# Exchanging the last two rounds of token blocks in an attention-and-experts kernel

## The chip, the cores and the metric

The kernel runs on one core of a Trainium2 chip. The metric is the device time of one execution in microseconds (us); a kernel's figure is the median of its runs. The engines are named as in the profile: PE is TensorE's matmul, PEld its weight load, DVE is VectorE, ACT is ScalarE, POOL is GpSimd, SP is SyncE (SPq is its DMA queue).

## The reference

A short convolution over time with softmax weights (7 taps, 8 heads) feeds a mixture of 8 experts. Every one of the 14336 tokens goes to its two best experts by noisy logits, and the two results are added with softmax weights:

```python
x = attn_out.reshape(B * S, D)                       # 14336 x 192
noisy_logits = x @ w_gate + np.log1p(np.exp(x @ w_noise)) * noise
top2 = np.argpartition(-noisy_logits, 2, axis=1)[:, :2]
...
h = np.maximum(x[mask] @ w1[e], 0.0)                 # 192 -> 1024
out[mask] += top2_w[mask, k, None] * (h @ w2[e])     # 1024 -> 192
```

## The kernel before

**Front end.** Tokens come in 14 chunks of 1024. For each chunk the kernel loads x, computes the convolution (DVE), splits it into a high and a low fp16 part, computes the gate logits (PE), picks the two experts, and scatters each token's record into the queues of its two experts in HBM (`xg`), with 16 indirect DMAs from POOL (line 411).

**Rounds.** After chunk c has been queued, round c takes one block of rows from each of the 8 experts' queues. `ROUNDS` lists the rounds as pairs (chunk after which the round may run, rows of a block). A queue gets 256 rows per chunk on the average, so there are 14 rounds of 256-row blocks; a fifteenth round of 128-row blocks takes what is left over. Where a queue holds fewer rows than a block, the block reaches back over rows that were taken already, and those are sent to spare rows behind the output. Whatever then remains would go through a loop of 128-row blocks (`leftovers`), which makes no pass on this data.

**One block.** SP loads the block's records (`metas`, 8 small DMAs per round, line 817) and its transposed rows (`rows`, tile xT, line 823; six buffers). A block has 8 slices of 128 hidden units, taken several at a time so that each step fills a 128x512 PSUM tile: four steps of two slices for a 256-row block, two steps of four slices for a 128-row block. Each step is: first layer on PE into pm (line 879), relu to fp16 on ACT (hi, line 894), the rest pm - hi on DVE (lo, line 898), second layer on PE into py (line 919). PE's program has the first layer run up to three steps ahead of the second. py is one PSUM tile per block, with **two buffers**: block n uses the buffer of block n-2. A 256-row block has two halves of 128 rows side by side in its py, called a and b below.

**Finishing a block.** For each half in turn, `finish` scales py by the gate into an SBUF tile y (ACT, line 931; six y buffers) and adds y into the output with an indirect accumulating DMA from POOL (line 936, behind a small memset, line 935). The adds of one block may follow each other at once; a block's first add waits until the adds of the block before have landed, since a token can be in both.

**What sets the order.** Nothing is scheduled on the chip. `Sched` runs every work stream as a generator that yields (engine, estimated us, function, what it depends on), keeps a clock per engine from these estimates, and writes the instructions into the engines' programs in the order in which it picks them. The engines then run these fixed programs in order, with semaphores between them. In `finish` the planner reaches the scale of half b only when it has placed the add of half a on POOL, so a planned backlog of POOL moves the scale of b down in ACT's program:

```python
ty = yield ("ACT", act(D) + 0.07, scale, [t0, ("g", o.c, o.e)] + ...)
if t == o.nt - 1:
    T["y", bi] = ty
ta = yield ("POOL", 1.85, add, [ty + (AL if o.c else 0.0), ...] + before("added", bi, 1), 0.27)
```

Below, the blocks of the round of 128-row blocks are M0 to M7, and those of the last round of 256-row blocks L0 to L7.

Of the kernel before, what the change touches and what calls it, by code (L numbers as in the profile page):

```python
# [33 lines left out]
NC = NJ // CH  # L34
PARTS = [[(0, 4), (4, 4)]] + [[(0, CH)]] * (NC - 1)
GT = 4
ROUNDS = [(c, 256) for c in range(NC)] + [(NC - 1, 128)]
BMAX = 256
RBUF = 3
NTM = BMAX // P  # L40
# [107 lines left out]
def moe_kernel(ctx, tc, x_lay, wgen, noise, wgn, w1, w2, xg, out):  # L148
# [25 lines left out]
    def dve(n):  # L174
        return (n / 0.96 + 155) / 1e3
# [60 lines left out]
    def before(key, i, n):  # L236

        return [(key, i - n)] if i >= n else []
# [198 lines left out]
    def routing(c):  # L437
# [106 lines left out]
        d = dve(8)  # L544
        for q, (cc, b) in enumerate(ROUNDS):
            if cc != c:
# [16 lines left out]
    def strays(q, t):  # L563

        V = nc.vector
        nt = ROUNDS[q][1] // P
        S = [P, E, nt]
# [214 lines left out]
    steps, blist = [], []  # L782
    for c, (_, b) in enumerate(ROUNDS):
        for e in range(E):
# [12 lines left out]
    def prologues():  # L797

        for c, (k, b) in enumerate(ROUNDS):
            base = []  # L800
# [40 lines left out]
    def gates(c, tm):  # L841

        nt = ROUNDS[c][1] // P
        S = [P, E, nt]
# [77 lines left out]
    def finish(bi, t0):  # L922
# [3 lines left out]
        for t in range(o.nt):  # L926
# [21 lines left out]
            if t == o.nt - 1:  # L948
                T["y", bi] = ty
            ta = yield ("POOL", 1.85, add, [ty + (AL if o.c else 0.0), ("clear", ROUNDS[o.c][0]), ("token", o.c)] + before("added", bi, 1), 0.27)  # L950
            T["add", n] = ta + 2.2
# [184 lines left out]
```

## Time and profile before

| | |
|---|---|
| median of 3 runs | 1201.41 us (1190.59 to 1201.69) |
| profiled execution | 1206.64 us, of which the span of the profile is 1204.7 us |
| PE busy | 1051.8 us, 87% of the span |
| DVE, ACT, POOL busy | 825.7 us (69%), 526.0 us (44%), 749.8 us (62%) |
| granted TensorE clock, mean | 0.95 |
| adds into the output (line 936) | 232, 1759 ns each |

The span runs from the first to the last instruction of the profiled execution; the execution's own time is 1.94 us longer. Busy shares are averages over the whole span: the first 100 us are loading and weight preparation, and the last 14 us have almost no PE work.

### The profile page before, as it was taken

Reading aid. Unit: us, or ns where it says so; the run is one execution under the profiler, and the core shown is the slowest. Engines: PE = TensorE matmul, PEld = TensorE weight load, DVE = VectorE, ACT = ScalarE, POOL = GpSimd, SP = SyncE. Lnnn points to the kernel's source line nnn. Section 1 sums busy time; section 2 is a strip of 40 time slices with the busy share of each in tenths; the row PEclk is TensorE's granted clock in tenths of the full one; section 3 lists DMA queues with packets and bytes.
Section 4 is the critical chain, followed back from the end, with each engine's and each line's share of the span. In section 5 each row is a group of like instructions: output and inputs, shape, how many; then the busy total and the mean of one; then the engine's idle time right before and its main releaser. Section 6 shows DMA issues by size and latency. Waiting matters only on the chain.

```text
span 1204.7 us, 27979 instructions
## 1 busy us (share of the span) xinstructions
PE 1051.8 (87%) x10862; PEld 953.8 (79%) x10862; DVE 825.7 (69%) x1552; ACT 526.0 (44%) x1191; POOL 749.8 (62%) x1013
## 2 busy tenths in 40 slices
PE   1414899797998999999999999989999889999995
PEld 0201499786997999889999889879898779999995
DVE  5898878686795969778887859678885343333331
ACT  6868573342443444443435344434343233333332
POOL 0004368477686868778684858778787867434333
PEclk9755999898998999999999999999999989999998
DMA  9993473665647577485748666365555545434341
GB/s 246 244 283 100 117 170 62 92 145 95 132 88 138 109 125 98 88 161 96 154 78 155 107 117 129 58 131 120 79 91 81 102 74 81 52 54 47 35 41 21
DMA packets 249686, 132.48 MB, mean 110 GB/s; under 512 B 182096, under 2 KB 242000, under 8 KB 247888
## 3 DMA queue, kind: packets, MB, share of 16 engines
q1 hardware_dynamic: 205392, 85.37, 32.3%
q0 software_dynamic: 44160, 45.31, 24.9%
q8 instruction: 85, 1.39, 0.5%
q14 instruction: 49, 0.40, 0.1%
HBM read 38.70 MB, written 58.10 MB: 80 GB/s over the span
## 4 chain that ended last, share of the span: by engine, by line
PE 52%; POOL 15%; DMA 10%; DVE 7%; issue 6%; ACT 6%; SPq 4%; another core or an unknown queue 0%; POOLq 0%; DVEq 0%; ACTq 0%
PE pm L879 27%; PE py L919 24%; POOL xg L411 8%; POOL out L936 7%; DMA xt<-x_lay 3%; DMA out<-y,token 3%; SPq L817 2%; DVE acc L337 2%; DVE tmp L327 2%; DVE lo L898 2%; DMA xg<-rec,pos 1%; DMA xT<-xg 1%; DMA wres<-w 1%; ACT junk L682 1%; ACT junk L273 1%
## 5 line engine op out<-in xcount | busy, mean ns | idle before, releaser
L879 PE MATMUL pm<-xT,wres 128*128 128x256 f16 (+1 forms) x4800 | 594.3, 271 | 30.2 <-DMA xT<-xg 23.4
L936 POOL DMA_INDIRECT out<-y,token x232 | 408.0, 1759 | 254.4 <-ACT y L931 89.3
L898 DVE SCALAR_TENSOR_TENSOR lo<-pm,hi 128x512 f16<-128x512 f32 x464 | 316.1, 686 | 301.1 <-ACT hi L894 261.4
L879 PEld LDWEIGHTS <-wres 128*128 128x128 f16 x4800 | 451.6, 99 | 83.4 <-DMA xT<-xg 21.9
L919 PE MATMUL py<-wres,hi 128*128 128x192 f16 x3712 | 503.3, 247 | 9.8 <-ACT hi L894 4.0
L894 ACT ACTIVATE hi<-pm 128x512 f16<-128x512 f32 x464 | 275.7, 596 | 507.4 <-PE pm L879 407.7
L919 PE MATMUL py<-wres,lo 128*128 128x192 f16 x1856 | 458.6, 247 | 4.5 <-issue 3.0
L919 PEld LDWEIGHTS <-hi 128*128 128x128 f16 x3712 | 341.6, 98 | 23.2 <-issue 8.9
L411 POOL DMA_INDIRECT xg<-rec,pos x224 | 292.0, 1304 | 76.4 <-issue 67.5
L919 PEld LDWEIGHTS <-lo 128*128 128x128 f16 x1856 | 182.3, 98 | 8.5 <-issue 5.5
L337 DVE TENSOR_TENSOR acc<-acc,tmp 128x1536 f32<-128x1536 f32 (+1 forms) x90 | 148.0, 1644 | 1.1
L327 DVE TENSOR_TENSOR tmp<-xt,wt 128x1536 f32<-128x1536 f32 (+1 forms) x90 | 148.2, 1646 | 0.7
L931 ACT ACTIVATE y<-py,gate 128x192 f32<-128x192 f32 x232 | 96.3, 417 | 78.0 <-PE py L919 37.6
L935 POOL MEMSET spacer<- 1x1 f32 x232 | 102.8, 443 | 0.1
L533 POOL TENSOR_SCALAR rec<-rr 128x8 f32<-128x8 f32 x14 | 3.2, 229 | 90.7 <-DVE rr L482 89.8
L410 POOL MEMSET spacer<- 1x1 f32 x224 | 53.3, 238 | 0.1
L273 ACT ACTIVATE junk<-xt 128x192 f16<-128x192 f32 x118 | 42.3, 359 | 23.9 <-DMA xt<-x_lay 22.0
L602 PE MATMUL sums<-ss,ones 128*128 128x2 f32 x32 | 8.1, 333 | 39.4 <-ACT junk L682 39.4
L602 PEld LDWEIGHTS sums<-ss,ones 128*128 128x128 f32 x32 | 7.1, 282 | 43.0 <-ACT junk L682 43.0
L739 PE MATMUL sums<-wres,dg 128*128 128x512 f32 (+1 forms) x48 | 29.3, 698 | 5.3 <-ACT wres L743 3.1
L352 DVE TENSOR_TENSOR rec<-acc,rec 128x512 f16<-128x512 f32 (+2 forms) x30 | 26.8, 900 | 3.1 <-ACT rec L348 2.7
L739 PEld LDWEIGHTS sums<-wres,dg 128*128 128x128 f32 x48 | 9.9, 230 | 22.3 <-ACT wres L743 10.4
(139 smaller groups left out, 514.8 us busy)
## 6 DMA issues: line engine op xcount, KB each, us to landing
xt<-x_lay SPq DMA_DIRECT2D x13, 1344.0 KB
out<-zrec SPq DMA_DIRECT2D x14, 768.0 KB
wres<-w SPq DMA_DIRECT2D x6, 768.0 KB
out<-y,token POOLq DMA_INDIRECT x232
xg<-rec,pos POOLq DMA_INDIRECT x224
wt<-wgen SPq DMA_DIRECT2D x14, 224.0 KB
wres<-w SPq DMA_DIRECT2D x6, 512.0 KB
wres<-w SPq DMA_DIRECT2D x12, 256.0 KB
```

The source lines that it names most:

```text
L273: nc.scalar.activation(q, xtile[s][:, i - first], AF.Square, accum_out=nrm[:, i:i + 1])
L327: V.tensor_mul(tm[key].rearrange("p j (h g) -> p j h g", h=H), xt[:, t:t + n].rearrange("p j (h g) -> p j h g", h=H), w[:, a:a + n].rearra ...
L337: ta = yield ("DVE", cc, lambda: V.tensor_add(tm["acc"], tm["acc"], tm["tmp"]), [])
L410: nc.gpsimd.memset(spacer, 0.0)
L411: i = nc.gpsimd.indirect_dma_start(out=xg, out_offset=bass.IndirectOffsetOnAxis(ap=idx, axis=0), in_=src, in_offset=None)
L879: nc.tensor.matmul(dst, w[:, c0:c0 + 128], m, start=i == 0, stop=i == 4)
L894: nc.scalar.activation(h[0][:, :n], pm[:, :n], AF.Relu)
L898: T["lo", si] = yield ("DVE", dve(n), lambda: nc.vector.scalar_tensor_tensor(h[1][:, :n], pm[:, :n], 0.0, h[0][:, :n], op0=OP.max, op1=OP. ...
L919: nc.tensor.matmul(dst, h[:, cols], w[:, c0:c0 + D], start=begin, stop=f == F // P - 1 and i == 2, skip_group_check=True)
L931: nc.scalar.activation(y[0], o.py[t // 2][:, (t % 2) * D:(t % 2 + 1) * D], AF.Copy, scale=gate_of[o.c][:, o.e, t:t + 1])
L935: nc.gpsimd.memset(spacer, 0.0)
L936: i = nc.gpsimd.indirect_dma_start(out=out, out_offset=bass.IndirectOffsetOnAxis(ap=token[o.c][:, o.e, t:t + 1], axis=0), in_=y[0], in_off ...
```

## The change

One list is written in another order: after 13 rounds of 256-row blocks the round of 128-row blocks now comes as the fourteenth, and the last round has 256-row blocks. Both wait for the last chunk, as before. The number and the shapes of all instructions stay as they are, and the queues end at the same row, so the leftover loop makes no pass either.

```diff
-ROUNDS = [(c, 256) for c in range(NC)] + [(NC - 1, 128)]
+ROUNDS = [(c, 256) for c in range(NC - 1)] + [(NC - 1, 128), (NC - 1, 256)]
+
```

The engines' programs are the same up to the first block of round 13; all lines behind the list have moved down by one. From there on the planner writes another order. Three places matter. In the rows, the numbers behind py, pm, hi and y tell the tiles apart.

ACT, in the last round of 256-row blocks, before: py_17069 and py_17188 are two neighbouring blocks. Both scales of a block stand together, with one relu between them.

```order
L931 ACTIVATE y0_17186<-py_17069,gate_15901 128x192
L894 ACTIVATE hi3_17201<-pm3_17174 128x512
L931 ACTIVATE y1_17206<-py_17069,gate_15901 128x192
L894 ACTIVATE hi4_17232<-pm4_17208 128x512
L894 ACTIVATE hi1_17273<-pm1_17239 128x512
L894 ACTIVATE hi2_17310<-pm2_17276 128x512
L931 ACTIVATE y4_17335<-py_17188,gate_15901 128x192
L894 ACTIVATE hi0_17350<-pm0_17313 128x512
L931 ACTIVATE y5_17355<-py_17188,gate_15901 128x192
```

ACT at the same place now: py_17002, py_17120 and py_17245 are L0, L1 and L2.

```order
L932 ACTIVATE y5_17231<-py_17120,gate_16931 128x192
L895 ACTIVATE hi4_17235<-pm4_17219 128x512
L932 ACTIVATE y2_17243<-py_17002,gate_16931 128x192
L895 ACTIVATE hi1_17281<-pm1_17258 128x512
L895 ACTIVATE hi2_17308<-pm2_17284 128x512
L895 ACTIVATE hi0_17335<-pm0_17311 128x512
L932 ACTIVATE y3_17352<-py_17245,gate_16931 128x192
L895 ACTIVATE hi3_17354<-pm3_17340 128x512
L932 ACTIVATE y0_17362<-py_17120,gate_16931 128x192
```

The scale of a block's half b has moved behind the scale of the next block's half a. It is so for L0 to L6; for L0 to L3 a relu stands between the two scales, as shown, and for L4 to L6 they stand next to each other.

PE, where a block's second layer begins, before (py_17188 is the last 256-row block):

```order
L879 MATMUL pm3_17174<-xT5_16727,wres_94 128x256
L919 LDWEIGHTS hi2_17144 [waits Activation_49]
L919 MATMUL py_17188<-wres_94,hi2_17144 128x192
L919 LDWEIGHTS hi2_17144
L919 MATMUL py_17188<-wres_94,hi2_17144 128x192
L919 LDWEIGHTS lo2_17145 [waits DVE_49]
```

PE where the second layer of L2 begins, now:

```order
L880 MATMUL pm4_17219<-xT0_16953,wres_94 128x256
L920 LDWEIGHTS hi0_17189 [waits Activation_49]
L920 MATMUL py_17245<-wres_94,hi0_17189 128x192 [waits Activation_49]
L920 LDWEIGHTS hi0_17189
L920 MATMUL py_17245<-wres_94,hi0_17189 128x192
L920 LDWEIGHTS lo0_17190 [waits DVE_49]
```

The first matmul into the py buffer has a wait for ACT of its own: the buffer is that of L0, whose half b is scaled by the third of the ACT rows above. It is the same for L2 to L7.

ACT at the end of the program, before (the last three blocks of the round of 128-row blocks):

```order
L931 ACTIVATE y5_17817<-py_17740,gate_16885 128x192
L894 ACTIVATE hi4_17832<-pm4_17795 128x512
L894 ACTIVATE hi1_17869<-pm1_17835 128x512
L931 ACTIVATE y2_17888<-py_17819,gate_16885 128x192
L931 ACTIVATE y3_17902<-py_17874,gate_16885 128x192
```

ACT at the end of the program now (py_17598 is L5, py_17711 is L6, py_17828 is L7):

```order
L932 ACTIVATE y1_17822<-py_17711,gate_16931 128x192
L932 ACTIVATE y4_17826<-py_17598,gate_16931 128x192
L895 ACTIVATE hi4_17841<-pm4_17810 128x512
L895 ACTIVATE hi1_17870<-pm1_17845 128x512
L932 ACTIVATE y5_17898<-py_17828,gate_16931 128x192
L932 ACTIVATE y2_17902<-py_17711,gate_16931 128x192
L932 ACTIVATE y3_17908<-py_17828,gate_16931 128x192
```

Three scales instead of two stand behind the last relu, and the second of them belongs to L6. POOL's adds stay in the order of the blocks: L6 a, L6 b, L7 a, L7 b.

## Rows read from the trace of the kernel before

**Rows 1.** Windows: us, busy us (x instructions) of each engine, granted clock, DMA share, GB/s.
```profile
1000.00:1190.80 190.80, 190.80 (x2178) 182.23 (x2175) 64.04 (x100) 71.67 (x138) 85.23 (x119) 1.00 0.39 48
1190.80:1204.70 13.90, 0.03 (x1) 0.00 (x0) 0.67 (x4) 0.42 (x1) 3.15 (x3) 0.61 0.18 20
```
**Rows 2.** Chain of work that ended last, final pieces: start, us, what.
```profile
1192.61 3.58 DMA out<-y,token
...
1196.94 1.56 POOL out L936
```
**Rows 3.** Timeline of POOL at the end: start, us, instruction [idle before, releaser].
```profile
1192.61 1.55 POOL L936 DMA_INDIRECT out<-y,token  x1 [2.67 <-DMA out<-y,token]
...
1196.94 1.56 POOL L936 DMA_INDIRECT out<-y,token  x1 [2.73 <-DMA out<-y,token]
```
**Rows 4.** Timeline of PE and ACT at the end.
```profile
1184.68 0.42 ACT L931 ACTIVATE y<-py,gate 128x192 f32<-128x192 f32 x1 [0.39 <-PE py L919]
...
1188.89 0.42 ACT L931 ACTIVATE y<-py,gate 128x192 f32<-128x192 f32 x1 [0.39 <-PE py L919]
...
1190.59 0.25 PE L919 MATMUL py<-wres,lo 128*128 128x192 f16 x1
1190.87 0.42 ACT L931 ACTIVATE y<-py,gate 128x192 f32<-128x192 f32 x1 [1.56 <-PE py L919]
```
**Rows 5.** Timeline of all engines where one 256-row block follows another.
```profile
1109.11 0.25 PE L919 MATMUL py<-wres,lo 128*128 128x192 f16 x1
...
1109.19 1.26 PE L879 MATMUL pm<-xT,wres 128*128 128x256 f16 x10
1109.39 0.42 ACT L931 ACTIVATE y<-py,gate 128x192 f32<-128x192 f32 x1 [0.39 <-PE py L919]
1110.09 1.56 POOL L936 DMA_INDIRECT out<-y,token  x1 [4.82 <-ACT y L931]
...
1110.28 0.33 PE L919 MATMUL py<-wres,hi 128*128 128x192 f16 x2
...
1110.48 0.60 ACT L894 ACTIVATE hi<-pm 128x512 f16<-128x512 f32 x1 [0.67 <-issue]
...
1110.97 0.41 ACT L931 ACTIVATE y<-py,gate 128x192 f32<-128x192 f32 x1
...
1111.27 0.93 PE L879 MATMUL pm<-xT,wres 128*128 128x256 f16 x7
1111.95 1.56 POOL L936 DMA_INDIRECT out<-y,token  x1 [0.26 <-issue]
```
**Rows 6.** Timeline of PE and ACT around the one wait of PE for a scale.
```profile
685.10 0.42 ACT L931 ACTIVATE y<-py,gate 128x192 f32<-128x192 f32 x1 [5.78 <-DMA out<-y,token]
...
685.57 0.48 PE L919 MATMUL py<-wres,hi 128*128 128x192 f16 x2 [2.42 <-ACT y L931]
...
687.44 1.93 PE L879 MATMUL pm<-xT,wres 128*128 128x256 f16 x10
...
689.21 0.33 PE L919 MATMUL py<-wres,hi 128*128 128x192 f16 x2
```
**Rows 7.** Windows after and among short gaps of PE, columns as in rows 1.
```profile
683.10:685.50 2.40, 0.04 (x1) 0.00 (x0) 0.68 (x1) 0.41 (x2) 2.18 (x3) 0.98 0.55 83
685.50:689.10 3.60, 3.53 (x22) 2.95 (x21) 2.81 (x4) 1.44 (x5) 3.15 (x6) 0.54 0.17 59
...
700.00:708.00 8.00, 6.37 (x65) 5.29 (x64) 4.86 (x17) 2.29 (x6) 5.46 (x9) 1.00 0.42 67
770.00:780.00 10.00, 8.37 (x79) 6.67 (x78) 4.51 (x16) 3.19 (x7) 8.53 (x13) 1.00 0.41 62
```
**Rows 8.** Timeline of PE between 700 and 708 us, its longest gap there.
```profile
704.66 0.17 PE L504 MATMUL bank<-th,tri 128*128 128x8 f16 x1 [0.98 <-DVE ln L490]
```
**Rows 9.** Timelines: SP's small loads of a round; POOL's wait for the gates.
```profile
1108.28 4.09 SPq L817 DMA_DIRECT2D meta<-xg  x8
...
1132.78 0.21 POOL L855 TENSOR_TENSOR gate<-gate,meta 128x8 f32<-128x8 f32 x1 [2.43 <-DVE gate L851]
```

## The prediction, made before the changed kernel ran

> **What bounds the kernel now.** I read the windows first. From 1000 us to 1190.8 us, the stretch that holds rounds 12 to 14, TensorE is busy for all of it at a granted clock of 1.00 [rows 1]; nothing else sets the pace there, so whatever makes PE wait in that stretch is paid in full, and whatever only moves work on ACT, DVE or POOL is free. The last 14 us are different: PE does nothing, and the chain of waits ends on POOL, add behind add [rows 1, 2]. The timeline of POOL shows why. In the round of 128-row blocks every block has one add, each must wait for the landing of the one before, and they come every 1196.94 - 1192.61 = 4.33 us [rows 3]. PE makes a block in 1188.89 - 1184.68 = 4.21 us [rows 4]. So POOL is a little behind, and the last block hurts most: it has no next block to share PE with, its scale starts only 1.98 us after the one before, and its add has to wait. Call E the end of the last matmul, 1190.59 + 0.25 = 1190.84 [rows 4]. The last add starts at 1196.94, that is E + 6.10, and the span ends 7.76 us later; that remainder stays as it is. The program splits so: what happens to E, and where the last add stands behind E.
>
> **What the change moves.** All instructions stay, with their sizes. Up to the first block of round 13 the programs are the same, so the sum has only the places below. PE's own work is the same sum in either order: 128-row steps cost what they cost, early or late.
>
> **Part 1, the tail by the sizes alone.** First as if ACT kept the old pattern, both scales of a block together. A scale starts 0.03 us behind the block's last matmul (1109.11 + 0.25 to 1109.39), an add 0.70 us behind the start of its scale (1109.39 to 1110.09), and the two adds of a block are 1.86 us apart (1110.09 to 1111.95) [rows 5]. Between the ends of L6 and L7 PE has two first-layer steps of 1.09 us (1109.19 to 1110.28) and four second-layer steps of 0.99 us (1110.28 to 1111.27) [rows 5], 6.14 us. L6 would add at E - 5.41 and E - 3.55, L7 a at 4.33 us behind that, E + 0.78, L7 b at E + 2.64. Against E + 6.10 that is a gain of 3.5 us. This is what the larger last block offers: two adds per wait instead of one.
>
> **Part 2, the tail by the program as written.** The order of ACT shown with the change is another: L5 b is scaled behind L6 a, L6 b behind L7 a. Let E6 be the end of L6, so E = E6 + 6.14. The scale of L6 a starts at E6 + 0.03, that of L5 b 0.42 us later, at E6 + 0.45, and L5 b's add at E6 + 1.15. POOL keeps the order of the blocks, so L6 a, though long scaled, goes 4.33 us behind it: E6 + 5.48 = E - 0.66. L6 b follows 1.86 us later at E + 1.20 (its scale starts at E + 0.45 and would allow E + 1.15). L7 a: E + 5.53. L7 b: E + 7.39. That is 1.29 us later than E + 6.10, so **+1.3 us** where part 1 promised -3.5.
>
> **Part 3, a new wait on PE.** py has two buffers, so the second layer of L2 writes where L0 was, and L0 b is now scaled behind L1 a and a relu. In the trace the same three ACT instructions stand at a block's end, only with the block's own half b as the third: scale at 1109.39, relu when the ten first-layer matmuls are through at 1110.48, scale at 1110.97 until 1111.38 [rows 5]. Before, nobody waited for that third one; the next block's second layer began at 1110.28 into the other buffer. Now it must wait until 1111.38. The lag from a scale's end to PE is 0.05 us (685.10 + 0.42 to 685.57, the one time that the trace has PE waiting for a scale) [rows 6]. So PE stands for 1111.43 - 1110.28 = 1.15 us. Queued behind the waiting matmul is all of PE's program: the next first-layer steps, hence relu, DVE and adds; nothing hides it, since PE was full. This happens where L2, L3, L4 and L5 begin. For L6 and L7 the two scales stand side by side and are done at 1109.39 + 2 x 0.42 = 1110.23, plus 0.05 that is the moment at which PE would begin: about nothing, at most 0.1 us each. Sum: 4 x 1.15 = **+4.6 us** on E. Bounds: 0 if something earlier already holds PE at these points, and 2.42 us a stall, the longest that a scale has cost (there ACT itself was held by an add) [rows 6], 9.7 us; I take 1.15 because rows 5 are the very instructions.
>
> **Part 4, things that move and stay covered.** (a) PE drains at the step from M7 to L0: the three last second-layer steps of the M round run without first layer between them, then three first-layer steps. The trace's own end has the same drain without a gap, and L0's hi and lo need 1.26 + 0.60 + about 0.7 us behind the start of its first step, against 3 x 1.09 = 3.3 us of matmuls. Nothing, but with 0.7 us of margin only. (b) SP: L0's rows go out behind eight small loads, 4.09 us [rows 9], once M2 is through the first layer; L0 is five blocks of 4.21 us = 21 us later, and those before it go at that pace too. Covered by some 15 us. (c) POOL's gates for the L round stand between the adds of M3 and M4 and wait for DVE, whose gate step stands behind the last lo of M7. In the trace a wait of the same kind cost POOL 2.43 us [rows 9]. Here it is longer: PE has 11.8 us of steps from the end of M3 to M7's last first layer (five pairs of 2.1 us and a step), then relu and lo, so M4 is added about 14.6 us behind the end of M3 instead of about 5. M5 to M7 follow at 4.33 us, L0 a at about 32 us, when its scale has waited 6 us; at L0 b POOL is level again. ACT has six y buffers, and the scale of L0 b needs that of M4, landed at about 18 us and wanted at 35. Covered; if it were not, ACT would hold the relus, and with them PE. (d) The M round's own lag of 0.12 us a block no longer meets the end.
>
> **The sum.** 4.6 + 1.3 = 5.9 us. On the profiled execution: 1206.64 + 5.9 = 1212.5 us. That execution lies 5.2 us above the median shown; the mechanism adds the same to any run, so on the median 1201.41 + 5.9 = **1207.3 us**, 0.5% slower. About 1%, 12 us, is what a measurement of this kernel can tell from no change: its three runs span 11 us.
>
> **Rivals.** *The tail shrinks and PE doesn't stall* (part 1 alone): 1201.41 - 3.5 = 1197.9 us. For it: the adds are the last chain, and the pairing is real. Against it: the programs are fixed, and scale b behind the next block's scale a is what stands in them; it would take a planner's order that the rows don't show.
>
> *The clock falls in the stalls*, the case that ends slower. After the gap of 2.42 us the granted clock was 0.54 for 3.6 us [rows 6, 7], that is mostly the lower level of 1.2 GHz: the second-layer step took 687.44 - 685.57 = 1.87 us for 0.99, the first-layer step 689.21 - 687.44 = 1.77 us for 1.09 [rows 6], 1.56 us lost. If each of the four stalls brings that, E moves by 4 x (1.15 + 1.56) = 10.8 us, and with the tail the sum is 12.1: 1213.5 us. Against it: between 700 and 708 us PE stood for 1.63 us in all, 0.98 of it in one piece, and between 770 and 780 us for 1.63 us in pieces; the clock stayed at 1.00 in both [rows 7, 8]. A stall of 1.15 us between full stretches of 8 us is nearer to these than to 2.42. It decides the sign beyond 1% only if it happens at all four.
> The Trainium skill, "TensorE: Matmul & The Clock Gate", section "A second HAM failure mode: psum-queue depth-cycling", speaks against the change: it tells of a kernel that cycles through PSUM banks, whose PE stands idle briefly between groups of matmuls often enough that the clock swings between its levels. Cycling through the py buffers with a stall in each block would be such a case, and by that rule the time is this rival's 1213.5 us; the windows at 700 and 770 us don't bear it out, and without it the sum stays 1207.3 us.
>
> *POOL's backlog holds ACT* (c above without its cover): each 1 us by which an add lands too late for its y buffer is 1 us of PE. The margin is about 17 us, so this needs adds of twice the length; some 1215 us or more.
>
> **How the numbers follow.** Stalls and longer tail, 1204 to 1211 us: 0.68. Shrunken tail without stalls, about 1198: 0.11. Clock falls in some or all stalls, 1209 to 1214: 0.14. Backlog or late rows: 0.03. The rest, 0.04, is a shift of the whole run such as the 1190.59 among the three. The range 1196 to 1214 takes in the first three. Beyond 1% slower (above 1213.4) I put 0.15: half of the clock's case, the backlog, and what the spread of runs lifts over the bound; beyond 1% faster 0.04; within 1% 0.81.
>
> **What would show it.** In the changed profile: four waits of PE for ACT's scale in the second layer of the last round, 1.0 to 1.3 us each, about 9.5 us apart, and a clock of 1.00 around them; the relus of that round evenly spaced otherwise; POOL waiting some 8 us for the gates in the M round with no wait of ACT for an add behind it; the last add 7.4 us behind the last matmul. Wrong would be: no such waits (rival one, or the planner's order matters less than I think), a clock below 1.00 between 1120 and 1195 us, or a gap of PE at the first block of the last round.

## The result, and the profile after

The changed kernel takes 1206.93 us against 1197.73 us of the kernel before (medians of 22 runs each). The medians lie 9.2 us apart. The ratio of the mean times is 1.0062 with a 95% interval of 1.0037 to 1.0087, that is 7.4 us slower (4.4 to 10.4). The forecast was 5.9 us.

The two profiled spans, 1204.7 and 1208.1 us, differ by less than that, because the front of the program happened to run faster in the one execution that was profiled of the changed kernel. The last block of round 12 is the same work in both; its first scale on ACT stands at 1092.73 us before and at 1087.55 us after. The first fence is the timeline of the kernel before, the second that of the changed kernel:

```profile
1092.73 0.42 ACT L931 ACTIVATE y<-py,gate 128x192 f32<-128x192 f32 x1 [0.39 <-PE py L919]
```
```profile
1087.55 0.42 ACT L932 ACTIVATE y<-py,gate 128x192 f32<-128x192 f32 x1 [0.39 <-PE py L920]
```

So the changed kernel enters the two exchanged rounds 5.2 us ahead, and the profile ends 3.4 us behind: from that point on it needs 8.6 us more. Only this stretch is compared below.

**PE.** Windows of the changed kernel, columns as in [rows 1]:

```profile
1000.00:1191.00 191.00, 186.25 (x2121) 177.18 (x2118) 62.33 (x98) 69.48 (x134) 82.82 (x118) 1.00 0.37 48
1088.00:1190.20 102.20, 98.22 (x1168) 93.73 (x1165) 32.08 (x48) 35.94 (x68) 35.81 (x47) 1.00 0.36 40
```

Where [rows 1] had PE busy without a break up to its last matmul, 102.20 - 98.22 = 3.98 us are now missing before it, at the same clock of 1.00. The timeline of PE has them in four pieces, all of them waits for the scale on ACT, and nothing else above 0.2 us:

```profile
1139.91 0.33 PE L920 MATMUL py<-wres,hi 128*128 128x192 f16 x2 [0.99 <-ACT y L932]
...
1149.40 0.32 PE L920 MATMUL py<-wres,hi 128*128 128x192 f16 x2 [1.00 <-ACT y L932]
...
1158.88 0.33 PE L920 MATMUL py<-wres,hi 128*128 128x192 f16 x2 [1.00 <-ACT y L932]
...
1168.36 0.33 PE L920 MATMUL py<-wres,hi 128*128 128x192 f16 x2 [0.99 <-ACT y L932]
```

The waits are 9.48 us apart. An undisturbed 256-row block takes 8.33 us, from one first scale to the next in the kernel before:

```profile
1117.71 0.42 ACT L931 ACTIVATE y<-py,gate 128x192 f32<-128x192 f32 x1 [0.39 <-PE py L919]
...
1126.04 0.42 ACT L931 ACTIVATE y<-py,gate 128x192 f32<-128x192 f32 x1 [0.39 <-PE py L919]
```

So each wait costs 1.15 us; the idle time shown is 1.00 because the matmuls ahead of it are shown to end about 0.16 us after the moment at which the next one could have started. Sum 4.6 us. ACT's side of the first one, in the timeline of ACT, is the pair of scales that stood at 1109.39 and 1110.97 in [rows 5], now of two blocks:

```profile
1137.86 0.42 ACT L932 ACTIVATE y<-py,gate 128x192 f32<-128x192 f32 x1 [0.39 <-PE py L920]
1139.45 0.41 ACT L932 ACTIVATE y<-py,gate 128x192 f32<-128x192 f32 x1
```

1139.45 + 0.41 = 1139.86, and PE goes on at 1139.91: the lag of 0.05 us of [rows 6].

**The tail.** The last matmul ends at E = 1189.98 + 0.25 = 1190.23. The timeline of POOL from the add of L5 b on answers to [rows 3]:

```profile
1189.98 0.25 PE L920 MATMUL py<-wres,lo 128*128 128x192 f16 x1
```
```profile
1185.13 1.56 POOL L937 DMA_INDIRECT out<-y,token  x1 [2.46 <-ACT y L932]
...
1190.85 1.56 POOL L937 DMA_INDIRECT out<-y,token  x1 [4.12 <-issue]
...
1192.71 1.56 POOL L937 DMA_INDIRECT out<-y,token  x1 [0.26 <-issue]
...
1197.02 1.55 POOL L937 DMA_INDIRECT out<-y,token  x1 [2.71 <-DMA out<-y,token]
...
1198.87 1.56 POOL L937 DMA_INDIRECT out<-y,token  x1 [0.26 <-issue]
```

The adds are L5 b, L6 a, L6 b, L7 a, L7 b. The last one starts at E + 8.64, where it was E + 6.10: 2.5 us. Within the chain, L7 a stands 4.31 us behind L6 b and the pairs are 1.86 us apart, as forecast; L6 a stands 5.72 us behind L5 b, 1.39 us more than the 4.33 of [rows 3]. The chain of work that ended last gives the time from the start of an add to its landing. For L5 b it is 4.65 us, against 3.55 and 3.57 for L6 b and L7 a:

```profile
1185.13 4.65 DMA out<-y,token
...
1192.71 3.55 DMA out<-y,token
1197.02 3.57 DMA out<-y,token
```

**The remainder.** From the start of the last add to the end of the span it was 7.76 us before and is 1208.1 - 1198.87 = 9.23 us now. The timeline of DVE shows what grew: the count of leftover rows, whose result every engine reads before the program ends. Before, then after:

```profile
1192.47 0.17 DVE L1038 TENSOR_TENSOR cnt<-run,con 128x8 f32<-128x8 f32 x1 [3.25 <-DMA out<-y,token]
```
```profile
1201.00 0.17 DVE L1039 TENSOR_TENSOR cnt<-run,con 128x8 f32<-128x8 f32 x1 [12.39 <-DMA out<-y,token]
```

Its tiles lie in memory that two of the six y buffers (y4, y5) hold until then. Before, the last user of these was the third block from the end; now it is L7 a (y5 in ACT's last rows), and the count waits for the landing of that add at 1197.02 + 3.57 = 1200.59. The price is 1.5 us. This too comes with the late scales and not with the exchange as such: the scale of L6 b, placed behind that of L7 a, makes L7 a's the third scale from the end, the one that gets y5. In e1, e3 and e6 below, exchanged as well, the count starts ahead of L7 a's add and the remainder is 7.75 to 7.9 us.

4.6 + 2.5 + 1.5 = 8.6 us, which is the whole difference of the two profiles behind round 12, and lies within the interval of the times.

### The profile page after: what moved, and what is told of

The parts are those of the page before. It is cut to its first block, busy times and chain, and to the rows that moved or that the text cites. A ratio compares the mean times of both kernels' runs of the same rounds, so it can differ in the third digit from the quotient of the medians.

```text
span 1208.1 us, 27972 instructions
## 1 busy us (share of the span) xinstructions
PE 1052.2 (87%) x10862; PEld 959.4 (79%) x10862; DVE 829.7 (69%) x1552; ACT 528.7 (44%) x1191; POOL 755.3 (63%) x1013
## 3 DMA queue, kind: packets, MB, share of 16 engines
q8 instruction: 85, 1.39, 0.5%
## 4 chain that ended last, share of the span: by engine, by line
PE 61%; DMA 11%; DVE 8%; POOL 8%; ACT 5%; SPq 4%; issue 3%; POOLq 0%; DVEq 0%; ACTq 0%
PE pm L880 32%; PE py L920 28%; DMA xt<-x_lay 4%; POOL xg L412 4%; POOL out L937 3%; DMA wres<-w 3%; DVE acc L338 3%; DVE tmp L328 3%; SPq L818 2%; DVE lo L899 2%; DMA out<-y,token 1%; ACT junk L274 1%; DMA xT<-xg 1%; DMA xg<-rec,pos 1%; ACT hi L895 1%
## 5 line engine op out<-in xcount | busy, mean ns | idle before, releaser
L920 PEld LDWEIGHTS <-hi 128*128 128x128 f16 x3712 | 342.3, 98 | 33.0 <-ACT hi L895 13.7
L920 PEld LDWEIGHTS <-lo 128*128 128x128 f16 x1856 | 182.7, 98 | 14.6 <-DVE lo L899 13.4
L740 PE MATMUL sums<-wres,dg 128*128 128x512 f32 (+1 forms) x48 | 32.9, 778 | 4.7 <-ACT wres L744 2.5
```

The lines of the kernel that those rows point to most:

```text
L920: nc.tensor.matmul(dst, h[:, cols], w[:, c0:c0 + D], start=begin, stop=f == F // P - 1 and i == 2, skip_group_check=True)
```

## The experiments

Theory A: the late scale of half b, which the planner writes in the last round, is the whole cost; the exchange itself would gain. Theory B: the exchange costs by itself (the drain of PE between the rounds, POOL's backlog behind the gates, larger loads), and the scales are a bystander. A third reading is the clock. The chips differ in absolute time (the kernel before had medians from 1198 to 1214 us), so ratios to the kernel before on the same chip are given, and lengths from the profiles: PE's waits, the last add behind E, and the remainder. "By lengths" means the sum of these three, less that of the kernel before.

**Both scales together (e1).** `finish` is rewritten so that a block of the last round yields its two scales first and then its two adds:

```diff
+        both = o.c == len(ROUNDS) - 1
...
-        for t in range(o.nt):
+        tiles = list(range(o.nt))
+        for part in ([("s", tiles), ("a", tiles)] if both else [(k, [t]) for t in tiles for k in "sa"]):
```

> The changed kernel, but in the last round the planner places both scales of a block before its two adds, so that half b is no longer scaled behind the next block's half a. Theory A (the late scale of half b is the whole cost): PE's four waits of about 1.0 us for a scale in the last round are gone, the last add starts about 2.6 us behind the last matmul (8.6 in the changed kernel, 6.1 before), the span ends about 7.8 us behind the start of the last add, and the time is about 3.5 us below the kernel before (ratio 0.997), 10 to 12 us below the changed kernel. Theory B (the exchange of the rounds itself costs: the drain of PE between the two rounds, POOL's backlog behind the gates, the larger loads) : the time stays 4 us or more above the kernel before (ratio 1.003 to 1.006), with PE waiting elsewhere between the end of round 12 and the end.

Measured: ratio 0.9971 (0.9930 to 1.0013). Windows and POOL's timeline:

```profile
1060.00:1199.00 139.00, 139.00 (x1629) 133.36 (x1628) 46.41 (x71) 52.24 (x100) 55.60 (x74) 1.00 0.36 42
```
```profile
1200.49 1.55 POOL L937 DMA_INDIRECT out<-y,token  x1 [2.78 <-ACT y L932]
...
1202.35 1.56 POOL L937 DMA_INDIRECT out<-y,token  x1 [0.26 <-SPq L1050]
```

PE has no gap; the last matmul ends at 1199.66, the last add starts at E + 2.69, and the span (1210.1 us) ends 7.75 us behind that. By lengths 3.4 us less than the kernel before. Theory B falls: drain, backlog and larger loads are all still there.

**A third py buffer (e2).** ACT's program stays as in the changed kernel; L2 and L5 write into another PSUM bank, so nobody waits for the late scale:

```diff
-            o.py = [psb.tile([P, 512], F32, name="py", bufs=2)]
+            if o.c == len(ROUNDS) - 1 and o.e % 3 == 2:
+                o.py = [psum.tile([P, 512], F32, name="bank")]
+            else:
+                o.py = [psb.tile([P, 512], F32, name="py", bufs=2)]
```

> The changed kernel with a third PSUM buffer for py in the last round (the bank that the gate logits no longer use), and ACT's program as it is in the changed kernel: half b is still scaled late, but no block writes where it stands. Theory A: no wait of PE for a scale in the last round, 4 x 1.15 = 4.6 us less than the changed kernel in the stretch of the last round (8.33 us from block to block instead of 9.48); the tail stays: last add 7.4 to 8.6 us behind the last matmul, end 9.2 us behind it. Time about 4 us above the kernel before (ratio 1.003). Theory B: the blocks of the last round stay 9.5 us apart where they were, or the time stays at the changed kernel's (ratio 1.006).

Measured: ratio 1.0039 (1.0005 to 1.0074). Windows, and POOL's timeline from L5 b to L6 a and at the end:

```profile
1062.00:1193.00 131.00, 131.00 (x1546) 125.80 (x1544) 43.52 (x67) 48.69 (x93) 49.22 (x66) 1.00 0.33 41
```
```profile
1188.10 1.56 POOL L940 DMA_INDIRECT out<-y,token  x1 [2.37 <-ACT y L935]
...
1193.85 1.56 POOL L940 DMA_INDIRECT out<-y,token  x1 [4.15 <-issue]
...
1201.80 1.56 POOL L940 DMA_INDIRECT out<-y,token  x1 [0.26 <-issue]
```

The four waits are gone, the first scales of L1 and L4 (1145.46 and 1170.44 us) are 8.33 us a block apart again, and the tail is untouched: E = 1193.20, last add E + 8.60, remainder 9.2 us. By lengths 3.9 us above the kernel before. The waits were those for the py buffer, and 4.6 us is their price by lengths; the times alone don't resolve it.

**The tail alone (e3).** The edit of e1 with `o.c == len(ROUNDS) - 1 and o.e >= 4`.

> The changed kernel with both scales of a block together only from the fifth block of the last round on: PE's four waits stay (second layer of L2 to L5), the end of the program gets the order of e1. Theory A: four waits of PE of about 1.0 us, 4.6 us in all; the last add starts about 4 us behind the last matmul instead of 8.6; the end comes 7.8 us behind that add instead of 9.2. Time about 2 to 3 us above the kernel before (ratio 1.002), 6 us below the changed kernel. Theory B: no less than the changed kernel (ratio 1.006).

Measured: ratio 1.0021 (0.9985 to 1.0057). PE waits three times, not four (1.00 us each, before L2, L3 and L4): the scale of L3 b now stands behind both scales of L4, and L5 takes L4's buffer, not L3's: PE begins L5's second layer at 1181.84 us, ahead of the scale of L3 b at 1182.54. (That the PSUM pool hands out the buffer that the program frees first fits this and wasn't tested.) Four waits were expected. The last add starts at E + 4.45 and the end follows 7.83 us later. By lengths 3 x 1.15 - 1.65 + 0.07 = 1.9 us above the kernel before. The direction is A's, the interval alone doesn't exclude 1.000.

**The count in memory of its own (e5).** The changed kernel, with cnt, cni and tot taken from the pool of the constants, so that they don't lie where y4 and y5 lay.

> The changed kernel with the three small tiles of the leftover count in memory of their own, so that DVE's count at the end need not wait until the y buffers of the last round are free. In the changed kernel that count starts at 1201.0 us, behind the landing of L7 a's add, and the span ends 9.2 us behind the start of the last add; before, the count was done at 1193.2 us and the end came 7.8 us behind the last add. If the count is what lengthens that remainder: count done before the last add has landed, the end 7.8 us behind the start of the last add, 1.5 us gained, which the times alone can't tell; PE's four waits and the last add at 7.4 to 8.6 us behind the last matmul stay. If the remainder is something else (the adds' landing by pairs): it stays at 9.2 us.

Measured: ratio 1.0076 (1.0040 to 1.0111), which doesn't resolve 1.5 us. The timeline of DVE:

```profile
1203.14 0.16 DVE L1040 TENSOR_TENSOR cnt<-run,con 128x8 f32<-128x8 f32 x1
```

The count is done while PE still works; the last add starts at 1213.54, E + 8.70, and the span ends at 1221.4, 7.86 us later instead of 9.23. So the remainder's growth was the count.

**Late scales in the old order of the rounds (e4).** The kernel before, where the scale of half b in its last round of 256-row blocks is made to wait, in the plan only, for the next block's scale of half a:

```diff
-            ty = yield ("ACT", act(D) + 0.07, scale, [t0, ("g", o.c, o.e)] + ([("add", u)] if u is not None else []))
+            ty = yield ("ACT", act(D) + 0.07, scale, [t0, ("g", o.c, o.e)] + ([("add", u)] if u is not None else [])
+                        + ([("ya", bi + 1)] if o.c == NC - 1 and t and o.e < E - 1 else []))
+            T["ya" if t == 0 else "yb", bi] = ty
```

> The kernel before, with the old order of the rounds, but in its last round of 256-row blocks the scale of half b is planned behind the next block's scale of half a, right next to it with no relu between. It separates the late scale from the exchange of the rounds. Theory A (PE stalls only where a relu stands between the two scales, and late adds lengthen POOL's chain): no wait of PE for a scale at L2 to L7, one of about 1 us at the second 128-row block, where the plan puts a relu between; POOL enters the 128-row round some 4.5 us later and can't catch up there, so the last add starts about 10.5 us behind the last matmul instead of 6.1. Sum 1.15 + 4.4 = 5.5 us above the kernel before, ratio 1.0046. If any late scale stalls PE (rival): seven to eight waits, 8 us or more on top, ratio above 1.010. If only the exchange of the rounds matters: ratio 1.000.

In the second version the dependence is `sch.after(("ya", bi + 1), 1.0)`, which puts a relu between the two:

> As the run before it, but with the scale of half b planned 1 us later still, so that a relu stands between the two scales at every block of that round, as it stands in the changed kernel at four. Theory A: eight waits of PE for a scale of about 1.0 us (L2 to L7 and the first two 128-row blocks), 8 x 1.15 = 9.2 us, at a granted clock of 1.00; the last add about 9.3 us behind the last matmul instead of 6.1; sum 12.4 us, ratio 1.010. If the clock fell in such stalls (rival): 8 x 1.56 = 12.5 us more, ratio 1.021, and the clock below 1.00 in that round. If only the exchange of the rounds matters: ratio 1.000.

Measured: side by side 1.0044 (1.0007 to 1.0081), with a relu between 1.0090 (1.0053 to 1.0127). Side by side PE never waits (the one wait that I expected at the second 128-row block didn't come, most likely by the same choice of buffer as in e3), and the last add starts at E + 9.99; by lengths 3.9 us, where 5.5 were expected. With the relu PE waits seven times, not the eight that I expected: again none at the second 128-row block. First and last of them in the timeline, and the window over them:

```profile
1125.40 0.32 PE L919 MATMUL py<-wres,hi 128*128 128x192 f16 x2 [1.00 <-ACT y L931]
...
1182.38 0.33 PE L919 MATMUL py<-wres,hi 128*128 128x192 f16 x2 [1.00 <-ACT y L931]
```
```profile
1115.00:1183.00 68.00, 61.02 (x664) 56.98 (x663) 20.64 (x32) 22.87 (x44) 21.86 (x30) 1.00 0.26 34
```

7 x 1.15 = 8.1 us, and the last add at E + 11.75, 5.7 us later than before: 13.7 us by lengths, 10.9 us (6.4 to 15.4) by the times. The last add was expected at E + 9.3; what makes this tail longer is not shown. Late scales cost in the old order of the rounds as well, and one relu between two scales decides whether PE stalls. The clock stays at 1.00 through seven stalls.

**One number of the planner (e6).** The changed kernel, where the planner expects an add of the last two rounds to land 1.0 us earlier:

```diff
-        T["added", bi] = ta + 2.6
+        T["added", bi] = ta + (2.6 if o.c < NC - 1 else 1.6)
```

> The changed kernel with one number of the planner changed: from the 128-row round on it plans the landing of an add 1.0 us earlier (1.6 instead of 2.6 us behind its issue), so that it no longer thinks POOL behind when it places the last round's scales; half b of a block then stands ahead of the next block's half a. The instructions are the same. Theory A: no wait of PE for a scale in the last round, the last add about 2.7 us behind the last matmul, the end 7.8 us behind that; 3.5 us below the kernel before, ratio 0.997. Theory B (the exchange itself costs): ratio 1.003 to 1.006.

Measured: ratio 0.9977 (0.9944 to 1.0009); no wait of PE, last add at E + 2.63, remainder 7.9 us. By lengths 3.3 us less than before. The window on PE, and ACT at the end of L1:

```profile
1056.00:1193.00 137.00, 137.00 (x1609) 131.46 (x1607) 46.11 (x70) 51.10 (x98) 54.54 (x74) 1.00 0.36 43
```
```profile
1137.95 0.42 ACT L932 ACTIVATE y<-py,gate 128x192 f32<-128x192 f32 x1 [0.44 <-PE py L920]
...
1145.73 0.92 ACT L932 ACTIVATE y<-py,gate 128x192 f32<-128x192 f32 x2
```

The late scale comes from the plan's backlog of POOL. The two scales of a block do not stand together here: that of L0 a is at 1137.95 us, that of L0 b 7.78 us later, just ahead of that of L1 a. PE begins L2 in L0's buffer only at 1147.12 us, when L0 b has been scaled, so nobody waits.

**The two again, side by side (e7, e8).** The kernel of e1 and the changed kernel, unaltered, in one set.

> The kernel of the first experiment again (exchanged rounds, both scales of a block together in the last round), for a narrower interval, side by side with the changed kernel. Theory A: ratio to the kernel before 0.997, with the upper end of the interval below 1.000 if the runs are many enough; some 10 us below the changed kernel.

> The changed kernel again, on the same chip and in the same call as the run before it. Ratio to the kernel before 1.006 as first measured; PE's four waits of 1.0 us, the last add 8.6 us behind the last matmul and the end 9.2 us behind that add, as in its first profile. Theory A by these lengths: 4.6 + 2.5 + 1.5 = 8.6 us above the kernel before, ratio 1.007.

Measured: e1's kernel 0.9959 (0.9928 to 0.9989), the changed kernel 1.0079 (1.0045 to 1.0112). The first is now clear of 1.000: with the planner's order mended, the exchange gains 4.9 us by the times (1.3 to 8.6) and 3.4 us by lengths; the two medians of this set are 1192.81 and 1205.70 us. The changed kernel's profile repeats its lengths: four waits of 1.0 us, last add E + 8.16, remainder 9.1 us.

| kernel | PE waits | last add behind E | remainder | sum, us | by the times, us |
|---|---|---|---|---|---|
| before | 0 | 6.10 | 7.76 | 0 | 0 |
| changed | 4 | 8.64 | 9.23 | +8.6 | +7.4 (4.4 to 10.4) |
| e1, together | 0 | 2.69 | 7.75 | -3.4 | -3.5 (-8.5 to 1.6) |
| e2, third py | 0 | 8.60 | 9.2 | +3.9 | +4.7 (0.6 to 9.0) |
| e3, tail alone | 3 | 4.45 | 7.83 | +1.9 | +2.5 (-1.8 to 6.9) |
| e5, count | 4 | 8.70 | 7.86 | +7.3 | +9.2 (4.9 to 13.5) |
| e4, side by side | 0 | 9.99 | 7.81 | +3.9 | +5.3 (0.8 to 9.8) |
| e4, relu between | 7 | 11.75 | 7.75 | +13.7 | +10.9 (6.4 to 15.4) |
| e6, plan | 0 | 2.63 | 7.9 | -3.3 | -2.8 (-6.8 to 1.1) |
| e7, e1 again | 0 | 2.66 | 7.79 | -3.4 | -4.9 (-8.6 to -1.3) |
| e8, changed again | 4 | 8.16 | 9.1 | +8.0 | +9.5 (5.4 to 13.4) |

The sum is 1.15 us per wait plus the differences of the two lengths from those of before. The times are the ratios' excess over 1 times the time of the kernel before on that chip. All ten sums lie within the intervals, which are 6 to 10 us wide; the shares of a sum rest on the profiles.

## Why the prediction was right

The mechanism was the forecast's: the planner's order, not the sizes of the blocks, decides, and part 1 (the gain of 3.5 us that the larger last blocks offer) is real but only e1 (with e7, the same kernel) and e6 collect it: their last add starts at E + 2.63 to E + 2.69, where part 1 had E + 2.64.

*Part 3, the wait on PE:* forecast four stalls of 1.15 us before L2 to L5, none before L6 and L7, at a clock of 1.00. Measured just so; e2 shows that they are for the py buffer, e4 that the relu between the scales makes them.

*Part 2, the tail:* right in kind, mis-sized. The last add was to start at E + 7.39 and starts at E + 8.64, since one add, L5 b's, took 4.65 us to land and the next one came after 5.72 us, where the sum has 4.33. The term is 2.5 us where the forecast had 1.3.

*The step that failed* is the sentence that the 7.76 us behind the last add stay as they are. They grew by 1.5 us, because the late scales also gave y5, whose memory the leftover count takes over, to L7 a, whose add is the last but one. I had followed the adds and the scales into the last round and not the buffers that the instructions behind it inherit. The two errors have the same sign: 8.6 us by lengths for 5.9. That the median of 1206.93 us lies so close to the 1207.3 us of the forecast is luck: the median before that it starts from, of three runs, was 3.7 us above that of all 22.

*Part 4, the covers:* all four held. PE shows no gap at L0; POOL waits 6.80 us for the gates in the M round (forecast some 8), and no scale waits for an add in this stretch:

```profile
1117.55 0.22 POOL L856 TENSOR_TENSOR gate<-gate,meta 128x16 f32<-128x16 f32 x1 [6.80 <-DVE gate L852]
```

*The rivals:* the shrunken tail without stalls did not come, as the program forbids it. The clock did not fall, in four stalls or in seven: the windows at 700 and 770 us of [rows 7] were the right neighbours, the gap of 2.42 us the wrong one. The Trainium skill, "TensorE: Matmul & The Clock Gate", section "A second HAM failure mode: psum-queue depth-cycling", tells of a clock that swings between its levels because PE stands idle briefly and often while it cycles through PSUM banks. The trace doesn't agree here: seven stalls in a row of 1.0 us each, one per block, left the clock at 1.00.

## What to carry to other kernels

Where a planner writes fixed programs, a change of sizes or order is costed from the program that comes out, not from the change: look at which instructions swapped places on each in-order engine, and who waits on a buffer that they free. Here an eviction of a PSUM buffer (a scale) that came behind another block's relu held TensorE for 1.15 us where the block that uses the buffer next was due. The same eviction right next to the other block's scale (e4), or as late as 7.78 us behind its twin but ahead of the buffer's next user (e6), cost TensorE nothing. Follow the last users of every buffer into the program's end: whatever runs there and inherits their memory waits for them, here 1.5 us.

## What was unexpected of the hardware

The add of L5 b took longer to land only in kernels where the chip fetched instructions by DMA while its rows were on the way. The DMA view of the changed kernel for 1185 to 1189 us shows it: the rows' queue (q0) and one packet of 0.02 MB in an instruction queue (q8), and the row of rates (GB/s in 40 slices of 0.1 us) ends in a thin trail.

```profile
GB/s 0 0 0 0 0 0 0 0 0 0 0 0 0 0 0 0 0 0 0 0 0 0 218 54 54 54 100 138 154 161 77 54 23 0 0 0 0 15 15 8
...
q0 software_dynamic: 140, 0.10, 23.7%
q8 instruction: 1, 0.02, 2.3%
```

The packet begins at 1187.3 us and ends at 1188.7 us; nothing of the rows moves from 1188.3 us on, and from 1188.7 us the last eight follow one by one, up to 1189.3 us. With such a packet in it, the next add came after 5.72, 5.75, 5.77 and 5.32 us (changed kernel, e2, e5, e8); in e3, without one in the same stretch, after 4.6 us.

Other adds in the last two rounds of the eleven profiles bear it out. In 14 of them (these four included) an instruction packet of this size began 2.0 to 2.9 us after the start of the add, while its rows were on the way, and the last row was through 3.9 to 4.4 us after that start each time. For 143 adds without an instruction packet among their rows (all whose rows can be told from those of a neighbour) the median is 3.2 us. A fetch isn't all that can hold an add up: the one at 1123.22 us in the changed kernel is followed after 5.32 us by the next without any instruction packet between them. No run removed the fetch, so that it is the cause is likely, but not shown.
